# Holding the x transposes and all later loads back until the first x chunk is copied, and copying the gate column earlier

## The chip, the cores and the metric

The kernel runs on one core of one Trainium2 chip. The metric is the device time of one execution in microseconds (us); less is better.

Names used below: PE is TensorE, DVE is VectorE, ACT is ScalarE, POOL is GpSimd and SP is SyncE. A "chunk" is 128 of the 2048 rows of x. A transfer is "issued" when SP or ACT begins the instruction that starts it, and "lands" when the last of its 16 semaphore steps arrives. Times inside a run count from the start of the profiled span.

## The reference, cut to what matters

```python
g = _sigmoid((x * gate_w).sum(-1, keepdims=True))
a = _A_ref(x, A_wqkv, A_wo)        # linear attention: q, k, v = x @ wqkv, ...
b = _B_ref(x, B_w1, B_w2, B_w3, B_w4)
return g * a + (1 - g) * b         # x is 2048 x 640
```

The change touches only the start of the kernel: K = x @ wk for all 16 chunks. The gate's dot product rides along as one extra column (index 640) of wk. After K comes Q = x @ wq, and then everything else.

## The kernel before

The contraction runs over the 640 features, so PE needs x transposed: `xT`, features on the partitions. Chunks 0 and 1 are turned by PE itself (`turn`); chunks 2 to 15 are turned on their way in by transposing DMAs, issued by SP right behind the weight loads.

```python
    load_x(0, 1)                                       # SP: x chunk 0
    aq.dma_start(g5[:], gate_w.rearrange("(c p) -> c p", p=P))
    load_wk(sp, 1)
    load_wk(aq, 0)
    load_x(1, 2, aq)                                   # ACT's queue: x chunk 1
    load_wk(sp, 3)
    load_wk(aq, 2)
    load_wk(sp, 4)
    for c0, c1 in ((2, 3), (3, 4), (4, 6), (6, 8), (8, 12), (12, 16)):
        load_xT(c0, c1)                                # one transposing DMA each
    sp.dma_start(wq_sb, wqkv_v[:, :, 0:D])
    # ... [cut: x, wv, w1, wo, w2, w3, all on SP]

    def turn(c):
        for pt, a, b in turns:                         # parts (0, 2) and (2, 5)
            # ... [cut: PE turns the 128x128 blocks of the part]
            if c == 0 and b == DC:
                nc.tensor.matmul(pt[:, 1, 0:DC], lhsT=g5z[:], rhs=ident[:, 0:DC], start=True, stop=True)
            nc.vector.tensor_copy(xT[:, a:b, c * P:(c + 1) * P], ...)
            if c == 0 and b == DC:
                nc.vector.tensor_copy(wk_sb[:, :, D], pt[:, 1, 0:DC])     # the gate column

    turn(0)
    warmup(1, TS)                                      # filler matmuls
    for n, dc in enumerate(k0_order):                  # K of chunk 0, part by part of wk
        if n == 3:
            turn(1)
        elif 1 <= n < 3:
            warmup(1, 2 * P)
        k_mm(kp, 0, (dc,), first=k0_order[0], last=k0_order[-1])
    k_evac(kp, 0)
    for c in range(1, NCH):                            # K of chunks 1 to 15: 10 matmuls each
        pt = pair()
        k_mm(pt, c, range(DC))
        k_evac(pt, c)
```

## Time and profile before

| | before |
|---|---|
| median time, first 3 runs | 264.6 us (264.48 to 264.68) |
| median, with 3 more runs taken beside the changed kernel | 264.45 us (264.15 to 264.68) |
| profiled execution | 264.31 us, span 262.6 us |

From the page, the span, PE's line of part 1, and the chain of work that ended last by engine:

```profile
span 262.6 us, 4246 instructions
PE 257.9 (98%) x1719; PEld 160.0 (61%) x1738; DVE 142.7 (54%) x282; ACT 82.7 (31%) x123; POOL 20.2 (8%) x65
...
PE 98%; issue 0%; DVE 0%
```

PE is busy all the time, and the chain that ended last is PE's own work. Such a kernel gets shorter only where PE waits or runs filler work. The waits view for PE (what it waited for, total us, times, longest) leaves one place of any size for that, the very start (the 0.2 us of the second line fall far behind the K stage):

```profile
PE pp L199 <- PEq L607: 0.8, 1, 0.8
PE pp L500 <- issue: 0.2, 1, 0.2
```

Line 199 is the filler. The chain of waits over the first 15 us (start, length, what) shows the fillers woven between the K matmuls (line 186) of chunk 0:

```profile
0.83 2.61 PE pp L199 x6
...
4.42 0.27 PE pp L186
4.69 0.03 issue
4.72 0.43 PE pp L186
5.14 0.21 PE pp L199
...
6.21 0.32 PE pp L214 x5
6.53 8.52 PE pp L186 x62
```

From 6.5 us on there is nothing on the chain but K matmuls. Chunk 1's first one starts at 6.99 us, and each chunk takes 1.362 us, without a gap, until Q starts at 27.42 us.

The second K matmul, at 4.72, needs the gate column. The timeline of DVE (start, length, engine, line, operation) shows the gate column last, after both parts of x:

```profile
3.69 0.89 DVE L219 CAST xT<-pp 128x256 bf16<-128x256 f32 x2 [1.28 <-PE pp L216]
4.49 0.17 DVE L222 CAST wk_sb<-pp 128x5 bf16<-128x5 f32 x1
```

The timeline of SP shows when the transposes are issued:

```profile
1.24 1.36 SPq L125 DMA_DIRECT2D wk_sb<-in_A_wqkv_dram  x3
2.65 14.00 SPq L122 DMA_TRANSPOSE xT<-in_A_x_dram  x6
```

And the windows view (us; busy time of PE, PEld, DVE, ACT, POOL with counts; granted clock; DMA share; GB/s) shows the DMA engines without a pause around these times. A share over 1 can only come from packets that overlap in time on an engine:

```profile
5.50:6.00 0.50, 0.50 (x5) 0.27 (x3) 0.00 (x0) 0.00 (x0) 0.00 (x0) 1.00 1.67 288
7.00:7.25 0.25, 0.25 (x4) 0.18 (x2) 0.00 (x0) 0.07 (x2) 0.00 (x0) 1.00 1.09 230
8.25:8.75 0.50, 0.50 (x5) 0.35 (x4) 0.39 (x2) 0.20 (x2) 0.00 (x0) 1.00 0.68 149
10.00:11.50 1.50, 1.50 (x14) 1.08 (x12) 1.29 (x3) 0.90 (x4) 0.00 (x0) 1.00 0.85 121
```

### The profile page before, as it was taken

Reading aid. Unit: us, or ns where it says so; the run is one execution under the profiler, and the core shown is the slowest. Engines: PE = TensorE matmul, PEld = TensorE weight load, DVE = VectorE, ACT = ScalarE, POOL = GpSimd, SP = SyncE. Lnnn points to the kernel's source line nnn. Section 1 sums busy time; section 2 is a strip of 40 time slices with the busy share of each in tenths; the row PEclk is TensorE's granted clock in tenths of the full one; section 3 lists DMA queues with packets and bytes.
Section 4 is the critical chain, followed back from the end, with each engine's and each line's share of the span. In section 5 each row is a group of like instructions: output and inputs, shape, how many; then the busy total and the mean of one; then the engine's idle time right before and its main releaser. Section 6 shows DMA issues by size and latency. Waiting matters only on the chain.

```text
span 262.6 us, 4246 instructions
## 1 busy us (share of the span) xinstructions
PE 257.9 (98%) x1719; PEld 160.0 (61%) x1738; DVE 142.7 (54%) x282; ACT 82.7 (31%) x123; POOL 20.2 (8%) x65
## 2 busy tenths in 40 slices
PE   8999999999999999999999999999999999999995
PEld 4777555788755644555577555567565577555553
DVE  2788778899947998955403464413356223112132
ACT  1555554321166236522502222412131332142200
POOL 5000050012210040001000001000001000000000
DMA  7999987016682566600132000051100051100011
GB/s 204 197 171 379 364 248 304 0 27 125 125 99 58 111 121 167 235 0 2 25 75 77 25 0 2 0 100 52 50 0 2 1 100 52 50 0 2 0 50 50
DMA packets 45757, 23.98 MB, mean 91 GB/s; under 512 B 35114, under 2 KB 44970, under 8 KB 45738
## 3 DMA queue, kind: packets, MB, share of 16 engines
q1 hardware_dynamic: 45296, 23.22, 35.1%
q10 hardware_dynamic: 442, 0.49, 0.5%
q8 instruction: 13, 0.21, 0.4%
q14 instruction: 6, 0.05, 0.1%
HBM read 12.21 MB, written 2.62 MB: 56 GB/s over the span
## 4 chain that ended last, share of the span: by engine, by line
PE 98%; issue 0%; DVE 0%
PE pp L500 22%; PE pp L467 21%; PE pp L186 9%; PE pp L315 8%; PE pp L451 8%; PE pp L420 8%; PE pp L349 8%; PE pp L243 8%; PE pp L199 1%; PE pp L387 1%; PE pp L475 1%; PE pp L509 1%; PE pp L368 1%; PE pp L258 0%; PE pp L216 0%
## 5 line engine op out<-in xcount | busy, mean ns | idle before, releaser
L467 PE MATMUL pp<-lnxT,w_sb 128*128 128x512 bf16 x249 | 59.8, 379 | 0.6
L500 PE MATMUL pp<-w_sb,h 128*128 128x384 bf16 (+3 forms) x414 | 57.6, 299 | 0.2 <-issue 0.2
L469 ACT ACTIVATE h<-pp 128x1024 bf16<-128x1024 f32 (+1 forms) x28 | 26.9, 961 | 82.2 <-PE pp L467 82.2
L500 PEld LDWEIGHTS <-h 128*128 128x128 bf16 x416 | 38.3, 98 | 19.3 <-issue 1.1
L467 PEld LDWEIGHTS <-w_sb 128*128 128x128 bf16 x260 | 25.4, 98 | 26.8
L514 DVE SCALAR_TENSOR_TENSOR oc<-pp,omg,x 128x640 bf16<-128x640 f32 (+2 forms) x20 | 14.4, 748 | 45.1 <-ACT h2x L478 21.3
L454 DVE SCALAR_TENSOR_TENSOR x<-pp,gate,x 128x640 f32<-128x640 f32 x16 | 13.9, 868 | 29.4 <-PE pp L451 29.4
L178 ACT ACTIVATE e<-pp 128x640 bf16<-128x640 f32 (+1 forms) x26 | 21.5, 826 | 9.6 <-PE pp L243 9.6
L451 PE MATMUL pp<-m_sb,pqT 128*128 128x320 bf16 x160 | 24.3, 299 | 0.0
L420 PE MATMUL pp<-w_sb,hsT 128*128 128x320 bf16 x160 | 23.9, 299 | 0.0
L423 DVE TENSOR_TENSOR x<-pp,x_sb 128x640 f32<-128x640 f32 x16 | 13.1, 820 | 19.7 <-PE pp L420 19.7
L186 PE MATMUL pp<-wk_sb,xT 128*128 128x320 bf16 (+1 forms) x160 | 23.1, 303 | 0.0
L315 PE MATMUL pp<-x_sb,pk 128*128 128x320 bf16 (+1 forms) x160 | 22.0, 300 | 0.0
L243 PE MATMUL pp<-xT,hsT 128*128 128x512 bf16 x98 | 21.6, 379 | 0.1
L315 PEld LDWEIGHTS <-pk 128*128 128x128 bf16 x160 | 18.8, 117 | 3.2
L420 PEld LDWEIGHTS <-hsT 128*128 128x128 bf16 x160 | 15.7, 98 | 8.2
L451 PEld LDWEIGHTS <-pqT 128*128 128x128 bf16 x160 | 15.7, 98 | 7.7
L186 PEld LDWEIGHTS <-xT 128*128 128x128 bf16 x160 | 15.7, 99 | 6.5 <-DVE xT L219 0.2
L349 PE MATMUL pp<-lnxT,w_sb 128*128 128x512 bf16 x76 | 17.9, 379 | 0.2
L243 PEld LDWEIGHTS <-hsT 128*128 128x128 bf16 x100 | 11.8, 118 | 9.7
L285 POOL TENSOR_SCALAR rstd<-mv 128x4 f32<-128x4 f32 (+1 forms) x11 | 3.4, 312 | 153.6 <-DVE mv L291 153.6
L180 DVE SCALAR_TENSOR_TENSOR pk<-pp,e 128x640 bf16<-128x640 f32 x16 | 13.2, 825 | 1.7
(76 smaller groups left out, 189.9 us busy)
## 6 DMA issues: line engine op xcount, KB each, us to landing
out_dram<-oc SPq DMA_DIRECT2D x14, 160.0 KB, 1.8
w_sb<-in_B_w_dram SPq DMA_DIRECT2D x1, 2160.0 KB, 8.4
w_sb<-in_B_w_dram SPq DMA_DIRECT2D x1, 2080.0 KB, 9.9
x_sb<-in_A_x_dram SPq DMA_DIRECT2D x1, 1280.0 KB
x_sb<-in_A_x_dram SPq DMA_DIRECT2D x1, 960.0 KB, 7.4
wo_sb<-in_A_wo_dram SPq DMA_DIRECT2D x6, 160.0 KB, 7.8
hsT<-in_A_wqkv_dram SPq DMA_DIRECT2D x1, 800.0 KB, 5.1
m_sb<-in_A_wqkv_dram SPq DMA_DIRECT2D x1, 800.0 KB, 12.0
```

Of the source, the lines that this page charges most:

```text
L178: nc.scalar.activation(ev, src, ACT.Exp)
L186: nc.tensor.matmul(pt[:, hf, 0:n], lhsT=xT[:, dc, c * P:(c + 1) * P], rhs=wk_sb[:, dc, hf * HD:hf * HD + n], start=(dc == first), stop=(dc ...
L243: nc.tensor.matmul(pt[:, t % 2, :], lhsT=wq_sb[:, dc, :].rearrange("p (m j) -> p j m", j=DC)[:, j], rhs=xT[:, dc, t * TS:(t + 1) * TS], st ...
L315: nc.tensor.matmul(pt[:, hf, 0:HD + hf], lhsT=w, rhs=x_sb[:, c, hf * HD:(hf + 1) * HD + hf], start=(c == 0), stop=(c == NCH - 1))
L349: nc.tensor.matmul(pt[:, i, :], lhsT=w, rhs=lnxT[t][:, dc, :], start=(dc == 0), stop=(dc == DC - 1))
L420: nc.tensor.matmul(pt[:, hf, 0:HD], lhsT=hsT[:, fc, 2 + c * P:2 + (c + 1) * P], rhs=w2_sb[:, fc, hf * HD:(hf + 1) * HD], start=(fc == 0), ...
L451: nc.tensor.matmul(pt[:, hf, 0:HD], lhsT=pqT[:, j, c * P:(c + 1) * P], rhs=m_sb[:, j, hf * HD:(hf + 1) * HD], start=(j == 0), stop=(j == D ...
L454: nc.vector.scalar_tensor_tensor(x1, pt[:, :, 0:HD], gate[:, c:c + 1], x1, op0=ALU.mult, op1=ALU.add)
L467: nc.tensor.matmul(pt[:, k, :], lhsT=w3_sb[:, dc, fc * P:(fc + 1) * P], rhs=lnT[:, dc, :], start=(dc == 0), stop=(dc == DC - 1))
L469: nc.scalar.activation(h2[:, 2 * i * TS:(2 * i + n) * TS], pt[:].rearrange("p h e -> p (h e)")[:, 0:n * TS], ACT.Gelu_apprx_tanh)
L500: nc.tensor.matmul(dst, lhsT=st[t]["h2"][:, fc * TS + cc * P:fc * TS + (cc + 1) * P], rhs=w4_sb[:, fc, a:b], start=start and fc == 0, stop ...
L514: nc.vector.scalar_tensor_tensor(oc[:, a:b], src, omg[:, c:c + 1], st[t]["x1"][cc][:, a:b], op0=ALU.mult, op1=ALU.add)
```

## The change

The intent is to let the first loads (two x chunks and five parts of wk), which gate PE's first K matmuls, have the DMA engines to themselves. The change does it without a new semaphore: a tiny DVE memset writes one column of `xT` that the first transpose will overwrite, so that transpose, and all SP loads behind it, must wait for DVE. The second half of the change moves the gate column's matmul and copy ahead of x chunk 0's second part.

```diff
     load_wk(sp, 4)
-    for c0, c1 in ((2, 3), (3, 4), (4, 6), (6, 8), (8, 12), (12, 16)):
-        load_xT(c0, c1)
-    sp.dma_start(wq_sb, wqkv_v[:, :, 0:D])
-    ... [cut: the other loads]
+
+    def late_loads():
+        for c0, c1 in ((2, 3), (3, 4), (4, 6), (6, 8), (8, 12), (12, 16)):
+            load_xT(c0, c1)
+        sp.dma_start(wq_sb, wqkv_v[:, :, 0:D])
+        ... [cut: the other loads, same order]
@@ in turn
-            if c == 0 and b == DC:
+            if c == 0 and a == 0:
                 nc.tensor.matmul(pt[:, 1, 0:DC], lhsT=g5z[:], rhs=ident[:, 0:DC], start=True, stop=True)
...
-            if c == 0 and b == DC:
+            if c == 0 and a == 0:
                 nc.vector.tensor_copy(wk_sb[:, :, D], pt[:, 1, 0:DC])
 
     turn(0)
+    nc.vector.memset(xT[:, 0:1, 2 * P:2 * P + 1], 0.0)
+    late_loads()
+    ... [cut: the w1x copies on POOL, moved here unchanged]
     warmup(1, TS)
```

More of the change, by code (lines that the diff above doesn't have):

```diff
@@ L134 @@
     load_wk(sp, 4)
-    for c0, c1 in ((2, 3), (3, 4), (4, 6), (6, 8), (8, 12), (12, 16)):
-        load_xT(c0, c1)
-    sp.dma_start(wq_sb, wqkv_v[:, :, 0:D])
-    load_x(2, 8)
-    load_x(8, 16)
-    sp.dma_start(wv_sb[:], wqkv_v[:, :, 2 * D:3 * D])
-    sp.dma_start(w1_sb[:], B_w1.rearrange("(c p) f -> p c f", p=P))
-    for g in range(NG):
-        sp.dma_start(wo_sb[:, g, :], A_wo[row0[g]:row0[g] + P, :])
-    for g in range(4):
-        sp.dma_start(w2_sb[:, g, :], B_w2[CG * g:CG * g + P, :])
-        sp.dma_start(w2_sb[32 * g:32 * (g + 1), 4, :], B_w2[CG * g + P:CG * (g + 1), :])
-    sp.dma_start(w3_sb[:], B_w3.rearrange("(c p) f -> p c f", p=P))
+    def late_loads():
+        for c0, c1 in ((2, 3), (3, 4), (4, 6), (6, 8), (8, 12), (12, 16)):
+            load_xT(c0, c1)
+        sp.dma_start(wq_sb, wqkv_v[:, :, 0:D])
+        load_x(2, 8)
+        load_x(8, 16)
+        sp.dma_start(wv_sb[:], wqkv_v[:, :, 2 * D:3 * D])
+        sp.dma_start(w1_sb[:], B_w1.rearrange("(c p) f -> p c f", p=P))
+        for g in range(NG):
+            sp.dma_start(wo_sb[:, g, :], A_wo[row0[g]:row0[g] + P, :])
+        for g in range(4):
+            sp.dma_start(w2_sb[:, g, :], B_w2[CG * g:CG * g + P, :])
+            sp.dma_start(w2_sb[32 * g:32 * (g + 1), 4, :], B_w2[CG * g + P:CG * (g + 1), :])
+        sp.dma_start(w3_sb[:], B_w3.rearrange("(c p) f -> p c f", p=P))
     nc.gpsimd.memset(mhalf[:], -0.5)
@@ L167 @@
         nc.gpsimd.memset(kvT[:, b:b + 2], 0.0)
-    for dc in range(DC):
-        for g in range(4):
-            nc.gpsimd.tensor_copy(w1x[:, dc, 32 * g:32 * (g + 1)], w1_sb[:, dc, CG * g + P:CG * (g + 1)])
     def phi(dst, src, n):
@@ L220, in turn @@
                                   ptb[:, 0:(b - a) * P].rearrange("p (c s) -> p c s", c=b - a))
-            if c == 0 and b == DC:
+            if c == 0 and a == 0:
                 nc.vector.tensor_copy(wk_sb[:, :, D], pt[:, 1, 0:DC])
     turn(0)
+    nc.vector.memset(xT[:, 0:1, 2 * P:2 * P + 1], 0.0)
+    late_loads()
+    for dc in range(DC):
+        for g in range(4):
+            nc.gpsimd.tensor_copy(w1x[:, dc, 32 * g:32 * (g + 1)], w1_sb[:, dc, CG * g + P:CG * (g + 1)])
     warmup(1, TS)
```

## The prediction

> **What bounds the kernel now.** TensorE. The page shows PE busy 257.9 of 262.6 us (98%), and the chain of waits is 98% PE. The waits view charges PE with about 1 us, nearly all before its first instruction. So a change at the start wins or loses only where PE waits or runs filler matmuls there, and passes that to the end one to one.
>
> **The head today (timeline; the trace's single instructions and packets).** PE runs fillers until the first x chunk lands (3.09 us), turns it (3.23), does the first K matmul at 4.22 and the second, which needs the gate column, at 4.72: DVE copies the first part, the second part (0.55 us), then the gate column (done 4.66). Then PE waits for loads: wk part 3 lands at 5.33, x chunk 1 at 6.03 (15 of its 16 pieces by 5.51), wk part 4 at 6.40, wk part 2 at 6.58. Chunk 1's K matmuls start at 6.99; from there PE runs 1.36 us a chunk without a gap. The x transposes are issued from 2.65, but their first 256-byte packet moves at 5.3, behind the wk loads; until 6.0 about 500 of them share the DMA engines with the ACT queue's loads. The Trainium skill ("DMA: Bandwidth & Descriptors", "Issuing engines are not separate DMA queues") says that both queues run on the same 16 engines and interleave; the trace agrees.
>
> **What the change does.**
> 1. The gate column's copy ends near 4.3 instead of 4.66, so the second K matmul starts about 0.25 us earlier. Alone it is worth little: loads gate PE afterwards.
> 2. A DVE memset of about 0.1 us, near 4.75, releases SP. The transposes are issued about 2.15 us later (2.65 to 4.8). The loads no longer share with them: 500 packets of about 25 ns over 16 engines is about 0.8 us (estimate). I expect x chunk 1 at about 5.6, wk parts 2 and 4 near 6.0, and chunk 1's K matmuls at about 6.55: 0.43 us gained.
> 3. Cost: later transposes. A lone one-chunk transpose took 1.2 us to issue, its first packet 1.17 us after the issue began (lnxT), so the first x packets come at about 6.0, only 0.7 later than before. Chunks 4 to 7 then arrive near 9.7 to 12.5 against needs of 10.6 and 13.3. Chunks 8 to 11 are tight: today they land at 16.44 and PE takes them at 16.49; it will want them at 16.05. Packets nearly stood still at 14.3 to 16.35, about when a 16 KB instruction fetch ran (13.7 to 15.6). If that recurs, PE waits 0 to 1 us. Later loads (wq lands 21.8, used at 27.4) have room.
> 4. GpSimd's order is unchanged.
>
> **Prediction.** Best case 264.15; with an expected wait of about 0.2 us for chunks 8 to 11: 264.3 us, range 263.8 to 265.4. Chances: faster by over 2% 0.01, within 2% 0.97, slower by over 2% 0.02.
>
> **What would show it.** Second K matmul before 4.6; x chunk 1 before 5.8; chunk 1's K matmuls at 6.5 to 6.6; first transpose issue near 4.8; PE without a gap before chunks 2, 4 and 8; after 27 us every PE piece shifted alike.
>
> **What would make it wrong.** Transposes limited by issue, shifting by the full 2.15 us: PE waits at chunks 4 and 8, about 266.5. Or x chunk 1's slow piece is not due to the transposes: no gain.

## The result, and the profile after

| | before | changed |
|---|---|---|
| median of 6 runs | 264.45 us (264.15 to 264.68) | 265.14 us (264.79 to 265.44) |
| ratio, 95% interval | | 1.0026 (1.0013 to 1.0039) |
| profiled execution | 264.31 us | 264.79 us |
| chunk 1's first K matmul | 6.99 us | 6.60 us |
| first Q matmul | 27.42 us | 27.89 us |

A ratio here is the mean time of one kernel's fast runs over the mean time of the other's of the same rounds, so it is not quite the ratio of the medians in the table. The verdict is "within 2%"; the interval says that the changed kernel is slower by a little.

The timeline of DVE shows both halves of the change at work: the gate column is copied second, at 4.04, and the memset ends at 4.67:

```profile
3.70 0.42 DVE L218 CAST xT<-pp 128x256 bf16<-128x256 f32 x1 [0.79 <-PE pp L217]
4.04 0.17 DVE L221 CAST wk_sb<-pp 128x5 bf16<-128x5 f32 x1
4.11 0.55 DVE L218 CAST xT<-pp 128x384 bf16<-128x384 f32 x1
4.61 0.06 DVE L224 MEMSET xT<- 128x1 bf16 x1
```

The second K matmul now starts at 4.55 instead of 4.72, x chunk 1 lands at 5.60 instead of 6.03, and chunk 1's K matmuls start 0.39 us earlier. But the waits view for PE has a new line:

```profile
PE pp L198 <- PEq L611: 0.8, 1, 0.8
PE pp L185 <- DMA xT<-in_A_x_dram: 0.7, 1, 0.7
```

PE waits for an x transpose. The view counts from the modelled end of the last matmul. From start to start the gap is 0.98 us (10.55 to 11.53), 0.85 us more than PE's own pace; that figure is used below. The gap stands before chunk 4. The chain of waits over the first 15 us shows what it hangs on:

```profile
3.70 0.42 DVE xT L218
4.12 0.09 DVE wk_sb L221
4.21 0.45 DVE xT L218
4.65 0.04 DVE xT L224
...
4.71 1.31 SPq L122
6.01 0.05 issue
6.06 1.26 SPq L122
...
7.37 4.12 DMA xT<-in_A_x_dram
11.49 0.05 issue
11.53 3.58 PE pp L185 x25
```

This is to be read from the bottom. PE's run of K matmuls from 11.53 was released by a transposing DMA (chunks 4 and 5) that was issued at 7.37 and landed 4.12 us later. It was issued that late because SP had to issue two transposes before it, 1.3 us each, and the first of those had been released by the memset. PE's work between 3.67 and 11.53, and with it the whole gain at the start, is no longer on the chain. Over the full span, the page's chain now reads:

```profile
PE 96%; DMA 2%; SPq 1%; DVE 1%; issue 0%
```

The windows show the price in the DMA engines. From 5.5 to 6.0 the loads are nearly through; then, while SP works through its issues, the engines stand idle:

```profile
5.50:6.00 0.50, 0.50 (x9) 0.39 (x8) 0.00 (x0) 0.00 (x0) 0.00 (x0) 1.00 0.20 69
7.00:7.25 0.25, 0.25 (x4) 0.20 (x2) 0.00 (x0) 0.25 (x1) 0.00 (x0) 1.00 0.00 0
8.25:8.75 0.50, 0.50 (x6) 0.38 (x4) 0.50 (x1) 0.50 (x2) 0.00 (x0) 1.00 0.11 22
10.00:11.50 1.50, 0.85 (x7) 0.39 (x4) 1.29 (x3) 0.90 (x3) 0.00 (x0) 1.00 0.85 161
```

At 7.0 to 7.25 the DMA share is 0.00, where it was 1.09 before. In the kernel before, the transposes of chunks 2 and 3 had been issued by 5.3 us, before the loads were done, so their first packet moved at 5.31, while the last loads were still coming in, and no pause followed. Now each one-chunk transpose is moved before the next one's first packet is ready. SP's timeline:

```profile
4.71 12.24 SPq L122 DMA_TRANSPOSE xT<-in_A_x_dram  x6
```

Issue and landing of each transpose, read from the trace's semaphore steps, with later repeats of both kernels (their runs follow below):

| chunks | issued before / changed | landed before (3 profiles) | landed changed (2 profiles) | PE wants them, changed, if it never waits |
|---|---|---|---|---|
| 2 | 2.65 / 4.71 | 7.21, 7.09, 7.32 | 7.43, 7.63 | 7.96 |
| 3 | 4.01 / 6.06 | 7.84, 7.99, 7.88 | 8.91, 9.59 | 9.32 |
| 4, 5 | 5.31 / 7.37 | 9.72, 9.70, 9.57 | 11.49, 11.68 | 10.69 |
| 6, 7 | 6.84 / 8.73 | 12.03, 11.30, 11.50 | 13.48, 13.32 | 13.41 |
| 8 to 11 | 8.50 / 10.44 | 16.44, 14.76, 14.38 | 16.25, 17.32 | 16.13 |

The delay at chunk 2 is small (0.2 us) and grows to 1.8 us at chunks 4 and 5, nearly the full 2.06 us of later issue. There the kernel before had 1.35 us in hand (landed 9.72, PE there at 11.07); the changed one is 0.8 us short.

### The profile page after: what moved, and what is told of

Its sections match the earlier page's. It is cut to its first block, busy times and chain, and to the rows that moved or that the text cites. A ratio compares the mean times of both kernels' runs of the same rounds, so it can differ in the third digit from the quotient of the medians.

```text
span 263.1 us, 4267 instructions
## 1 busy us (share of the span) xinstructions
PE 258.9 (98%) x1738; PEld 159.9 (61%) x1738; DVE 142.7 (54%) x283; ACT 82.7 (31%) x123; POOL 20.2 (8%) x65
## 4 chain that ended last, share of the span: by engine, by line
PE 96%; DMA 2%; SPq 1%; DVE 1%; issue 0%
PE pp L504 22%; PE pp L471 21%; PE pp L319 8%; PE pp L424 8%; PE pp L455 8%; PE pp L353 8%; PE pp L247 8%; PE pp L185 6%; DMA xT<-in_A_x_dram 2%; PE pp L391 1%; PE pp L479 1%; PE pp L198 1%; PE pp L513 1%; SPq L122 1%; PE pp L372 1%; PE pp L262 0%
## 5 line engine op out<-in xcount | busy, mean ns | idle before, releaser
L471 PE MATMUL pp<-lnxT,w_sb 128*128 128x512 bf16 x260 | 60.4, 379 | 0.0
L353 PE MATMUL pp<-lnxT,w_sb 128*128 128x512 bf16 x80 | 18.1, 379 | 0.0
```

Source lines behind the costliest of these rows:

```text
L353: nc.tensor.matmul(pt[:, i, :], lhsT=w, rhs=lnxT[t][:, dc, :], start=(dc == 0), stop=(dc == DC - 1))
L471: nc.tensor.matmul(pt[:, k, :], lhsT=w3_sb[:, dc, fc * P:(fc + 1) * P], rhs=lnT[:, dc, :], start=(dc == 0), stop=(dc == DC - 1))
```

## The experiments

The theory, called A in the expectations, has two halves: the gain at the start is that the loads don't share the DMA engines with the transposes, and the loss is that PE waits for the later transposes, whose issue now sets their pace. Rivals: the gain is that of the gate column's order (B); or the wait at chunk 4 does not follow from the late issue, but from something in the two-chunk transpose itself.

All kernels here computed the right result. Four ran on one chip (e1 to e4), eight on another (e6 to e13), each job beside the kernel before: 264.32 us median on the first (264.03 to 264.69, 9 runs), 264.75 to 264.82 on the second, where before scattered more (264.07 to 266.44).

The K stage makes the accounting close. In every profile the first Q matmul starts at (chunk 1's start) + 15 x 1.362 us + (PE's waits between chunks), within 0.05 us, and the profiled execution took 236.9 us more than that start (236.88 to 236.98 in all 14 profiles). So one table holds all profiled executions; the waits are start-to-start gaps less 1.362:

| kernel | first transpose issued | chunk 1 starts | PE's waits (before chunk) | first Q matmul | this execution | median, ratio to before (95%) |
|---|---|---|---|---|---|---|
| before | 2.65 | 6.99 | none | 27.42 | 264.31 | 264.45 |
| e10 before again | 2.66 | 6.94 | none | 27.38 | 264.26 | 264.46, 0.9993 (0.9959 to 1.0028) |
| e13 before, third | 2.65 | 7.06 | none | 27.50 | 264.39 | one run |
| changed | 4.71 | 6.60 | 0.85 (4) | 27.89 | 264.79 | 265.14, 1.0026 (1.0013 to 1.0039) |
| e11 changed again | 4.71 | 6.78 | 0.12 (3), 0.74 (4), 0.18 (8) | 28.27 | 265.19 | 265.23, 1.0015 (0.9991 to 1.0039) |
| e1 gate only | 2.66 | 7.29 | none | 27.73 | 264.61 | 264.65, 1.0013 (1.0000 to 1.0026) |
| e2 hold only | 4.72 | 6.56 | 0.20 (3), 0.77 (4), 0.61 (8) | 28.59 | 265.49 | 265.49, 1.0045 (1.0032 to 1.0057) |
| e3 split 4, 5 | 4.71 | 6.54 | 0.58 (3), 0.82 (6), 0.99 (8) | 29.39 | 266.37 | 266.54, 1.0087 (1.0074 to 1.0101) |
| e4 all single | 4.71 | 7.17 | 0.12 (3), 1.19 (9), 1.03 (Q) | 29.95 | 266.88 | 266.54, 1.0087 (1.0073 to 1.0101) |
| e6 pair alone | 4.71 | 7.51 | 1.20 (6), 1.53 (8) | 30.68 | 267.57 | 266.64, 1.0063 (1.0028 to 1.0098) |
| e7 released earlier | 4.26 | 7.02 | 0.10 (4), 0.34 (8) | 27.91 | 264.82 | 264.74, 0.9999 (0.9976 to 1.0023) |
| e8 pair 2, 3 | 4.71 | 7.52 | 0.30 (2) | 28.27 | 265.21 | 265.16, 1.0013 (0.9989 to 1.0037) |
| e9 both | 5.09 | 7.52 | 0.50 (2) | 28.47 | 265.43 | 264.72, 1.0002 (0.9977 to 1.0026) |
| e12 held longer | 6.76 | 6.71 | 1.76 (2), 1.11 (4) | 30.02 | 266.91 | 267.12, 1.0097 (1.0062 to 1.0133) |

### e1: the gate column's half alone

```diff
-            if c == 0 and b == DC:      # both places in turn, in the kernel before
+            if c == 0 and a == 0:
```

> The kernel before with only the gate column moved ahead of the second part; loads are not held. Theory A (the head gain of 0.38 us comes from the loads no longer sharing the DMA engines with the transposes, the loss from PE's wait for x chunks 4 and 5): second K matmul at about 4.5 instead of 4.72, but x chunk 1 still lands near 6.0 and chunk 1's K matmuls still start at about 6.95 to 7.0, so the time is within 0.15 us of before, and no gap at chunk 4. Rival B (the gate order gives the head gain): chunk 1's K matmuls start at about 6.6 and the time falls by about 0.35 us.

The second K matmul started at 4.49, but chunk 1 at 7.29: x chunk 1 landed at 6.08, wk parts 4 and 2 at 6.71 and 6.88. No gap later. The time did not fall; its median is 0.33 us over before, where at most 0.15 was expected, and it lies at the edge of being 0.1% slower. The later landing of the wk parts would explain that for the profiled execution; why they landed later is not shown. Rival B falls: the gate order gains nothing while loads gate PE.

### e2: the hold alone

```diff
-            if c == 0 and a == 0:       # both places in turn, in the changed kernel
+            if c == 0 and b == DC:
```

> The changed kernel without the gate move: loads held, gate column copied last as before. Theory A: x chunk 1 lands at about 5.6, chunk 1's K matmuls start at 6.6 to 6.7, the transposes are issued at about 4.75, PE waits 0.8 to 1.0 us before chunk 4, and the time is 0.5 to 0.9 us over before, as the full change. Rival B: chunk 1's K matmuls start at about 6.95, and the time is about 0.4 us worse than the full change, 1.1 us over before.

Chunk 1 started at 6.56, as early as with the full change, and PE waited 0.77 us before chunk 4, about as expected, and at chunks 3 and 8 too. So the gain at the start (in this profile) and the loss both come with the hold. The time missed: the median is 1.17 us over before, where A expected 0.5 to 0.9. That is the number of rival B (1.1), but not by B's way, a late chunk 1; here the waits are longer, 1.58 us in all. Whether its 0.0019 over the full change's ratio is real stays open: the two were not in one job, and chunks 8 to 11 landed at 17.63 here, which scatters.

### e12: hold longer

```diff
     turn(0)
-    nc.vector.memset(xT[:, 0:1, 2 * P:2 * P + 1], 0.0)
-    late_loads()                        # and the w1x copies
...
             turn(1)
+            nc.vector.memset(xT[:, 0:1, 2 * P:2 * P + 1], 0.0)
+            late_loads()                # and the w1x copies
```

> The full change with the release moved behind the copies of x chunk 1, so that the transposes are issued at about 6.4 to 6.9 instead of 4.71. If issue time sets when x chunks land (theory A), every landing moves by the same 1.7 to 2.2 us, PE waits first at chunk 2 (lands at about 9.3 against a need of 7.96) and in all 1.7 to 2.2 us more than in the full change: 266.6 to 267.4 us, or 2.2 to 2.9 over before. If the landing at chunk 4 is set by something that does not move with the issue: under 1 us more.

SP's timeline and PE's waits in this kernel:

```profile
6.76 12.31 SPq L122 DMA_TRANSPOSE xT<-in_A_x_dram  x6
```

```profile
PE pp L185 <- DMA xT<-in_A_x_dram: 2.5, 2, 1.6
```

Issue moved by 2.05 us against the changed kernel. Chunk 2 landed 2.26 us later (9.69), chunks 4 and 5 2.13 us later (13.62), and the Q matmuls started 2.13 us later. This is the cleanest test of the loss: beyond what is in hand, each microsecond of later issue is about a microsecond of time.

### e7: release earlier

```diff
                 nc.vector.tensor_copy(wk_sb[:, :, D], pt[:, 1, 0:DC])
+                nc.vector.memset(xT[:, 0:1, 2 * P:2 * P + 1], 0.0)
...
     turn(0)
-    nc.vector.memset(xT[:, 0:1, 2 * P:2 * P + 1], 0.0)
     late_loads()
```

> The full change with the memset that releases the transposes moved ahead of the second part's copy: issue at about 4.2 instead of 4.71. Theory A: all transposes land about 0.5 us earlier, PE's wait at chunk 4 shrinks from 0.85 to about 0.35 us, their first packets move at about 5.5, when nearly all of the loads' packets are through, so the head gain stays at 0.25 to 0.4 us: 0.1 to 0.6 us under the full change, level with before. If the wait at chunk 4 does not follow the issue time, the time stays as with the full change.

SP's timeline and PE's waits:

```profile
4.26 12.72 SPq L122 DMA_TRANSPOSE xT<-in_A_x_dram  x6
```

```profile
PE pp L185 <- DMA xT<-in_A_x_dram: 0.2, 1, 0.2
```

The transposes were issued 0.45 us earlier, and the median fell by 0.4 to 0.5 us against the changed kernel (265.14 and 265.23), to the level of before. The size is as expected, but it is not clear of noise: these medians come from different jobs, and in one job two sets of the kernel before alone lay 0.36 us apart (264.46 in e10 against 264.82). The profiled execution got there by another road than expected: chunk 1 was late (7.02) and the waits small. The gain at the start was not kept in it. Chunks 4 and 5 landed earlier than in the two profiles of the changed kernel (11.16 against 11.49 and 11.68), as expected; chunk 2 landed later (8.03 against 7.43 and 7.63) and chunk 3 no earlier (9.53 against 8.91 and 9.59), which was not. Their first packet moved at 5.66, among the last loads.

### e3 and e4: smaller transposes

```diff
-        for c0, c1 in ((2, 3), (3, 4), (4, 6), (6, 8), (8, 12), (12, 16)):
+        for c0, c1 in ((2, 3), (3, 4), (4, 5), (5, 6), (6, 8), (8, 12), (12, 16)):   # e3
+        for c in range(2, NCH):                                                       # e4
+            load_xT(c, c + 1)
```

> The full change, but the transpose of chunks 4 and 5 issued as two of one chunk each. If the wait is that of a two-chunk transpose whose last packets dribble in for 1 us after the bulk: chunk 4 lands near 10.1 and chunk 5 near 11.5, so no wait there (needs 10.69 and 12.05). The next pair (6, 7) is then issued at about 10.0 instead of 8.73 and lands at 13.8 to 14.7 against a need of 13.4: PE's wait moves to chunk 6 and is 0.4 to 1.3 us; the time stays 0.1 to 0.9 us over before. If splitting costs nothing (the packets, not the issue, set the pace): pair (6, 7) still lands near 13.5 and the time is about 0.3 us under before.

> The full change, with all 14 transposes of one chunk each. Each should take 1.3 us to issue and land 2.75 us after its issue began, as chunks 2 and 3 did, which just keeps up with PE's 1.36 us a chunk: no wait at chunks 2 to 15, K stage over at about 27.0. SP is then free only at about 23.3 for the wq load, which lands at 26.5 to 28.5 against a need of about 27.0: PE waits 0 to 1.5 us before the first q matmul. Time between 0.4 us under and 1.1 us over before. If instead the transposes are slow for a cause other than their size, PE waits at chunk 4 again.

Both came out 2.2 us over before (266.54 against 264.32), worse than expected. In e3 the wait at chunk 4 went and came back at chunk 6 (0.82 us), as expected. Chunk 4 landed at 10.96, later than expected, but PE was not there before. What was not expected are the waits at chunk 3 (0.58 us; it landed 3.73 us after its issue) and at chunk 8 (0.99; issued 1.0 us later than in the changed kernel because of the extra issue, and landed at 18.43). In e4 each transpose but one took about 1.28 us to issue, as expected, and PE kept pace up to chunk 8, save 0.12 us at chunk 3. Then chunk 9 landed 5.36 us after its issue: from 16.25 to 17.5 us the trace shows at most 36 packets started in each quarter of a microsecond, against about 285 at full flow, while the engines count as busy. The wq load, at the end of the longer issue chain, cost the expected wait before Q (1.03 us). So splitting does not help. Each further transpose puts some 1.3 us of issue before whatever stands behind it: that is the later issue behind e3's waits at chunks 6 and 8, and e4's late wq load. But half of e4's loss, at chunk 9, is the standstill of the packets (see e6), and e3's wait at chunk 3 is a late landing; the issue time does not explain these.

The assumption that a one-chunk transpose always lands 2.75 us after its issue was wrong as well. It held for chunk 2, whose data was through before the next transpose's began (2.72 to 2.94 in the kernels released at 4.71 or later that issue it alone); later ones mostly took 2.9 to 3.9.

### e8 and e9: fewer issues

```diff
-        for c0, c1 in ((2, 3), (3, 4), (4, 6), ...):
+        for c0, c1 in ((2, 4), (4, 6), ...):           # e8; e9 has e7's release too
```

> The full change with chunks 2 and 3 in one transpose. Issuing a pair took 1.32 us where nothing held it up, as much as a single (1.31), so this takes one issue of 1.3 us out of the chain: pair (4, 5) is issued at about 6.05 and lands at 9.0 to 10.2, before PE wants it at 10.69. Pair (2, 3) is issued at 4.71 and lands at 7.5 to 8.6 against a need of 7.96: PE waits 0 to 0.65 us at chunk 2. Time 0.4 us under to 0.3 us over before. Rival (issue does not set the pace): pair (4, 5) lands at 11 or later again and the time stays at 0.7 us over before.

> Both: release at about 4.2 and chunks 2 and 3 in one transpose. Pair (2, 3) lands at 7.0 to 8.1 against a need of 7.96, pair (4, 5) at 8.5 to 9.7 against 10.69: no wait or at most 0.2 us. Chunk 1's K matmuls start at 6.6 to 6.75. Time 0.2 to 0.4 us under before, if chunks 8 to 11 land by 16.1.

With one issue less, pair (4, 5) was issued 1.19 us earlier than in the changed kernel (6.18 against 7.37) and landed 0.95 us earlier (10.54), and no wait is left there. This is the test of the issues themselves: the release was at 4.71 as in the changed kernel, and only one issue was missing. But the pair (2, 3) landed at 9.13, 4.42 us after its issue and outside the expected range, so the wait moved to chunk 2. The chain of waits in e8 says it in one line:

```profile
4.71 4.42 DMA xT<-in_A_x_dram
9.13 0.05 issue
9.18 4.94 PE pp L185 x35
```

The time stayed over before by 0.4 us in the medians, not clear of noise. In e9 the profiled execution was an unlucky one: the last piece of x chunk 0 came only at 4.04, which delayed the copies and the release to 5.09. Its other five runs took 264.62 to 264.75. In ratio it equals before. No version beat the kernel before.

### e6: is the two-chunk transpose slow by itself?

```diff
-    late_loads()                        # was: all transposes, then the other loads
+    first_xT()                          # chunks 2, 3 and the pair (4, 5)
...
         k_evac(pt, c)
+        if c == 1:
+            nc.vector.memset(xT[:, 0:1, 6 * P:6 * P + 1], 0.0)
+            late_loads()                # the rest, and the w1x copies
```

> A diagnosis, not a candidate: the full change, but the transpose of chunks 6 and 7, and all loads after it, are held until chunk 1's last DVE operation, so that nothing follows the pair (4, 5) in the queue while it is in flight. Theory A1 (the pair lands late because the next transpose is let in behind it and the two hold each other up): the pair is issued at 7.4 and lands at 10.1 to 10.5 instead of 11.49, with no wait at chunk 4; the next pair is issued at about 10.3 and lands at 13.5 to 15, so PE waits 0 to 1.5 us at chunk 6. Rival A2 (a two-chunk transpose is slow by itself): the pair still lands at 11.2 to 11.6 and PE waits 0.6 to 0.9 us at chunk 4.

The answer lies between the two, nearer to A2. With nothing behind it, the pair landed 3.78 us after its issue (all 16 pieces between 10.95 and 11.15); in the changed kernel it took 4.12 and 4.31 us, seven pieces at 10.70 to 10.81 and nine at 11.27 to 11.49 in the first profile. So the next transpose costs the pair 0.3 to 0.5 us, as far as one profile of the pair alone can tell, and the rest is its own: about 1.4 us from issue to its first packet, some 1.9 us of packets, and about half a microsecond from the last packet to the landing. PE did not wait at chunk 4, but only because chunk 1 was late here (7.51), so that PE wanted chunk 4 at 11.6; the landing at 11.15 would have missed the need of 10.69. The held pair (6, 7) was issued only at 11.18, and PE waited 1.20 us for it.

What makes packets stand still (in the kernel before from 14.8 to 16.3 us) is not settled, but the traces hold a suspect. In 11 of the 14 profiles there is, after 13 us, a stretch of 0.5 to 1.5 us in which at most 40 packets of the transposes start in each quarter of a microsecond, and each time it begins 0.5 to 1.9 us after the start of an instruction fetch of 16 KB (before: fetch at 13.68, standstill from 15.0; e2: 19.02 and 19.5; e4: 15.25 and 16.25). Of the other three, e3 comes close to it (35 to 50 packets, 1.2 us after its fetch), and in the changed kernel and e12 the fetch came when nearly all transposing packets had started (18.25 and 20.38). A milder slowing in e2 (16.5 to 17.5 us, 17 to 101 packets) had no fetch near it. No run moved the fetch, so that it is the cause is not shown.

### e10, e11 and e13: is the gain at the start real?

Both kernels were run again unchanged, because chunk 1's start scattered between kernels with the same head.

> The kernel before, run again for a second profile, because in the profiles so far chunk 1's K matmuls start at 6.54 to 7.52 us in kernels that hold the transposes and all have the same head, against 6.99 and 7.29 in the two that do not. If the head gain of the hold is real (theory A), this profile shows chunk 1 at 6.95 or later and later than that of the changed kernel in this same job; if the head is only scatter, either may be first. Time: a ratio of 1.000 within 0.002.

> The changed kernel again. Theory A: 0.3 to 0.9 us over before, chunk 1 at 6.5 to 6.9, and a wait at one or two of chunks 3, 4 and 8 of 0.7 to 1.3 us in all, which together with chunk 1's start give the whole difference to before at the first q matmul. If the head gain was scatter: chunk 1 at 7.0 to 7.5, and the waits at chunks 4 and 8 shrink by as much, so that the q matmuls start at about 27.9 all the same.

> A third profile of the kernel before, for the same question as the second: chunk 1 at 6.95 or later if the hold's head gain is real; no wait of PE at any chunk of the K stage.

In this one job chunk 1 started at 6.78 in the changed kernel and at 6.94 and 7.06 in the one before: a gain of 0.16 to 0.28 us, with the sign of theory A. Over all profiles it is not clean. The four without the hold lie at 6.94 to 7.29 (mean 7.07). The eight with the changed kernel's release or a later one and both x chunks on time (changed, e2, e3, e4, e6, e8, e11, e12) lie at 6.54, 6.56, 6.60, 6.71, 6.78, 7.17, 7.51 and 7.52 (mean 6.92). In the late three, wk parts 4 and 2 landed at 6.4 to 6.9 and 6.9 to 7.2, against 5.9 to 6.0 and 6.2 to 6.4 in the others. Why these loads are late in some executions is not settled, so a gain at the start is likely but not shown to be dependable.

The same runs correct one reading of the first profile: chunks 8 to 11, which landed 0.05 us before PE wanted them (16.44 against 16.49), landed at 14.76 and 14.38 in the repeats, with 1.7 and 2.2 us in hand. The first profile had caught a standstill there. It is not a rare one: in e1, which does not hold the loads either, they landed at 16.37, with 0.45 us in hand. In these two profiles the instruction fetch started earlier (13.68 and 13.85) than in the repeats (14.75 and 14.40).

## Why the prediction was right or wrong

The measured 265.14 us lies in the predicted range of 263.8 to 265.4, and "within 2%" was given 0.97. The centre, 264.3, was 0.84 us too low, and on the wrong side of before: it seems to be reckoned from the median of the first three runs, 264.6 (its best case is that less 0.43, rounded), so a gain of 0.3 us was predicted and a loss of 0.7 us measured (264.45 to 265.14). That the total still lies in the range is in part luck: the range had room for a wait of up to 1 us at chunks 8 to 11, and a wait of that size came at chunk 4, for another reason.

1. *PE bounds the kernel and a shift at the start passes to the end one to one.* Right. The first Q matmul shifted by 0.47 us and the last matmul by 0.47 us (259.67 to 260.15); over 14 profiles the rest took 236.9 us.
2. *The gate column alone is worth little.* Right: e1 shows no gain. The second K matmul started at 4.55, "before 4.6" as predicted.
3. *The hold frees the loads: chunk 1's K matmuls at about 6.55, 0.43 us gained.* Right in the profile it was checked on (6.60, 0.39 us). In the repeat it was 0.16 to 0.28 us, and in three of eight profiles of the held head there was none. (The trace before has 398 transposing packets until 6.0, not about 500.) As the Trainium skill ("DMA: Bandwidth & Descriptors", "Issuing engines are not separate DMA queues") says, both queues' packets share the engines; before, 59 packets of ACT's queue and 48 of SP's started in the quarter of a microsecond from 5.25, and in the changed kernel the DMA share of 5.5 to 6.0 us falls from 1.67 to 0.20 when the transposes are taken out of it.
4. *The first x packets come only 0.7 us later.* Nearly: the first moved at 6.12 instead of 5.31, 0.81 later, and chunk 2 landed only 0.22 us later.
5. *"Chunks 4 to 7 then arrive near 9.7 to 12.5 against needs of 10.6 and 13.3."* This is the step that failed. They arrived at 11.49 and 13.48. The needs were right (10.69 and 13.41); the landing was mis-sized by 1.8 us for the pair (4, 5). By the prediction's own terms (release at 4.8, two issues of 1.2 us, so the pair's issue at 7.2) 9.7 left 2.5 us from its issue to its landing; it was issued at 7.37 and took 4.12. I had added the issue time, 1.2 us to the first packet and a full-speed transfer of 1.1 us. I left out the half microsecond from the last packet to the landing, took a two-chunk transfer to run at the rate of the best stretches (it took some 1.9 us, e6), and allowed nothing for the transpose behind it (0.3 to 0.5 us, e6 against the changed kernel).
6. *"An expected wait of about 0.2 us for chunks 8 to 11."* The term was 0.85 us in the profiled execution, all at chunk 4, and 1.04 us in the second profile, 0.74 of it at chunk 4. The tight place was picked from one profile that had caught a standstill there; two more put the slack of before at chunks 8 to 11 at 1.7 us or more, more than the 1.35 at chunk 4. The worry was not empty, though: PE did wait at chunk 8 in e2, e3, e6, e7 and e11 (0.18 to 1.53 us).
7. *What would make it wrong: "transposes limited by issue, shifting by the full 2.15 us".* This came true in good part. The landing of the pair (4, 5) shifted by 1.77 of 2.06 us; e12 shows the slope, 2.13 us at the first Q matmul (1.9 to 2.0 in the medians) for 2.05 us of issue, and e7 the other direction.

The sum: predicted -0.43 + 0.2, so about -0.2; in the profiled pair -0.39 + 0.85 = +0.46, as measured (0.47). Behind it stands what the sum hides: once PE waits for a transpose at chunk 4, the gain before that point is worth nothing at all, as the chain shows. The changed kernel's chain runs from the copies of x chunk 0 over the memset and SP's issues to that landing; the loads that were sped up are not on it. e8 fits this, though its transposes differ: the gain at the start was missing (chunk 1 at 7.52), the wait was shorter, and the time was the same, 265.16.

## What to carry to other kernels

Before holding a load back to relieve an earlier one, work out for each transfer behind it when it would land and when it is wanted, with the whole time from issue to landing and not the transfer rate, and compare with the slack in more than one profile. A queue that is filled early hides the issue time of its later entries; a hold takes that cover away, and several short issues in a row may then set the pace. And a gain upstream of a new wait counts for nothing: ask whether the work that became faster is still on the chain.

## What the Trainium skill lacked or had wrong

- "DMA: Bandwidth & Descriptors", "Issuing engines are not separate DMA queues", calls the sequencer's time to initiate a DMA "usually small relative to the DMA itself". For transposing DMAs of x it was not: 1.26 to 1.31 us of issue per one-chunk transpose (128 rows of 640). In the changed kernel the DMA engines had moved chunk 2 and stood idle (share 0.00 at 7.0 to 7.25 us) before the issue of chunk 3 was over at 7.32. A two-chunk transpose cost 1.32 us to issue where nothing held it up, so the price is per transpose more than per byte.
- The same page, "DMA Transpose (X-bar)", gives no time from issue to landing, and no page looked up here gives one for blocks as large as these. Measured: a one-chunk transpose (128 x 640) landed 2.72 to 2.94 us after the start of its issue where its data was through before the next one's began, a two-chunk one 3.78 us alone and 4.12 to 4.31 us with another transpose right behind.
- No page looked up here tells that the packets of transposes can nearly stand still: at most 36 started in a quarter microsecond in e4 at 16.25 to 17.5 us, against about 285 in full flow. In 11 of 14 profiles a stretch of at most 40 began 0.5 to 1.9 us after the start of a 16 KB instruction fetch; the cause is open.
- No page looked up here gives a scatter of landing times for equal programs. The last wk part of the held head landed anywhere from 6.2 to 7.2 us, and chunks 8 to 11 of the unchanged kernel at 14.38, 14.76 and 16.44.
